# Sliding-window attention beside an S5 scan: the sum over eight shifts moved from VectorE into accumulating DMAs

## The chip, the cores and the metric

The kernel runs on one core of one Trainium2 chip. The metric is device time in microseconds (us); the time before is 157.37 us, the median of three runs (157.35 to 158.69). A run of this kernel is one launch with all inputs and the output in device memory.

The engines have the names of the profile: PE is TensorE (matmuls), PEld its weight loads, DVE is VectorE, ACT is ScalarE, POOL is GpSimd, SP is SyncE. Each engine works through its own queue in order and waits on semaphores for the others. Matmul results lie in PSUM, in eight banks that the kernel hands out one by one.

## The reference, cut to what matters

Two independent parts are put side by side in the output, 448 columns each, for a sequence of 2048 tokens.

```python
# part A: attention over W = 8 earlier tokens, spaced by 2; 16 heads of 28
q, k, v = split(x @ wqkv)
idx = pos[:, None] - 2 * arange(8)[None, :]
logits = einsum("bhsd,bhswd->bhsw", q, k[idx]) * 28 ** -0.5     # masked where idx < 0
attn = softmax(logits)
o = einsum("bhsw,bhswd->bhsd", attn, v[idx])
a = o.reshape(B, S, 448) @ wo
# part B: a diagonal complex state space model (S5)
h[t] = Lam_bar * h[t-1] + B_bar @ x[t]
y = 2 * real(C @ h) + x * Dskip
out = concatenate([a, y], axis=-1)
```

The change concerns the second einsum of part A: for each token and head, eight value vectors ("shifts") are weighted and added up.

## The kernel before, in words

**Layout of part A.** Sixteen neighbouring tokens lie on one partition, so 128 partitions hold all 2048. The keys and values have a halo of 14 tokens copied from the partition before, and a shift by two tokens is then only another offset along the free dimension. Queries, keys and values come from `proj` (L358 to L397), called with a matrix (0 for q, 1 for k, 2 for v), a range of token positions `j`, and a list of functions to be put between the positions. Each position takes three matmuls of 128 rows (L384) and one of 64 rows (L375), the 64-row tile. With `flip=True` the 64-row tiles go first, otherwise last; calls alternate so that 64-row tiles of two calls meet. ACT copies every finished bank to SBUF (L370). The functions in between are transposes of x (`g_xta`), products of the SSM's input weights (`b_weights`, L404, copied by ACT at L406), transposes of B's x (`b_x`, copied at L418), or single ScalarE steps (`act`).

**The value stage.** Tokens are handled in eight pairs, p = 0 to 7. For each pair VectorE multiplies the eight shifted value rows by the attention weights (`pv_mul`, L671): eight slices of 2 x 448 = 896 elements, in one buffer of eight slices or two of four (`where`, L650). Some products are then added together on VectorE (`joins`, L651, L677). `av` (L682 to L702) adds the slices that are left: TensorE multiplies each by an identity matrix, seven matmuls a slice, accumulating in two banks, which also transposes the result. ACT copies the sum to `oTs` (L702). `wo` (L709 to L726) multiplies by the output weights, for two pairs at a time behind av(2), av(4) and av(6), and singly for the pairs 6 and 7 at the end, and stores each half pair (112 KB).

The slices left for TensorE are 4, 6, 6, 7, 7, 7, 8 and 6 for the pairs 0 to 7, 51 in all. VectorE makes ten adds for that: one of four slices (pair 0) and nine of one slice.

**What sets the order.** The order on each engine is the order in which the program issues the instructions. TensorE's is written out by hand. VectorE's work is mostly a list of items with estimated costs (`add`), from which `pe()` and `pump` take items whenever the estimated load of TensorE is ahead. The products of the pairs 4 and 5 lie in the buffers of the SSM state, and wait until its last outputs have been issued (`free`). Pair 6 uses pair 0's buffer again, and pair 7 pair 1's (`pv_ok`).

POOL builds constants early and sets a few masked logits to -1e30 (L597); it issues no DMA in the kernel before. SP issues nearly all DMAs, the stores of the output among them.

Of the kernel before, what the change touches and what calls it, by code (L numbers as in the profile page):

```python
# [10 lines left out]
ALU = mybir.AluOpType  # L11
# [19 lines left out]
def view(ap, offset, dims):  # L31

    return bass.AP(ap.tensor, ap.offset + offset, [list(ap.ap[0])] + [list(d) for d in dims])
# [3 lines left out]
def kernel(  # L37
# [18 lines left out]
    V = nc.vector  # L56
    ACT = nc.scalar
    PE = nc.tensor
    POOL = nc.gpsimd
# [7 lines left out]
    def bank(dt=F32):  # L67
        return psum.tile([128, 512 if dt == F32 else 1024], dt, tag="b", name="b")
# [79 lines left out]
    ident = const.tile([128, 128], BF16, tag="ident")  # L148
# [32 lines left out]
    count = [0, 0, 0]  # L181
# [3 lines left out]
    def add(cost, fn, ok=None):  # L185
        todo.append((cost, fn, ok))
        return todo[-1]

    def pop():
        c, fn, _ = todo.pop(0)  # L190
        fn()
        load[1] += c

    def pump(lead=0.0):
        while (todo and load[1] < load[0] + lead and (todo[0][2] is None or todo[0][2]())
               and (not until or load[1] + todo[0][0] < until[0])):
            pop()
# [14 lines left out]
    def pe(cost):  # L212
        load[0] += cost
        pump(1.0)
# [144 lines left out]
    def proj(t, hi, n, *between, odd=False, flip=False):  # L359


        todo_ = list(between)
        js = range(hi, hi - n, -1)
        pss = {j: bank() for j in js} if flip else {}

        def copy(j):
            src = pss[j][:, 0:D].rearrange("p (h d) -> p d h", h=H)
            dst = (q_s[:, :, j * H:(j + 1) * H] if t == 0 else
                   k_s[:, :, HALO + j, :] if t == 1 else v_s[:, HALO + j])
            ACT.copy(dst, src)  # L370

        def halves_():
            for j in js:
                rows = slice(HS * (j % 2), HS * (j % 2 + 1))
                PE.matmul(pss[j][:, 0:D], xTA[rows, j // 2, 6, :], wts[rows, t, 3, :], start=flip, stop=not flip)  # L375

        if flip:
            halves_()
            pe(0.24)
        for j in js:  # L380
            if not flip:
                pss[j] = bank()
            for kt in range(3):
                PE.matmul(pss[j][:, 0:D], xTA[:, j // 2, 2 * kt + j % 2, :], wts[:, t, kt, :],  # L384
                          start=(kt == 0 and not flip), stop=(kt == 2 and flip))
            if flip:
                copy(j)
            pe(0.56)
            if (odd or j % 2 == 0) and todo_ and j > js[-1]:
                todo_.pop(0)()  # L390
        if not flip:
            halves_()
            for j in js:
                copy(j)
            pe(0.2 + 0.1 * n)
        for fn in todo_:
            fn()  # L397


    def b_weights(t):  # L400
# [242 lines left out]
    PD = 2 * D  # L643
# [4 lines left out]
    spare = (u1[:, 7 * D:7 * D + 4 * PD], wbuf[:, 0:4 * PD], BT.rearrange("p t k n -> p (t k n)"),  # L648
             tab.rearrange("p a t c -> p (a t c)"))
    where = ((kA,), (kB, lB), spare[0:2], spare[2:4], (uA[:, 0:4 * PD], uA[:, 4 * PD:]), (uB,), (kA,), (kB, lB))  # L650
    joins = {(0, 0): 4, (1, 0): 1, (1, 1): 1, (2, 0): 1, (2, 1): 1, (3, 0): 1, (4, 0): 1, (5, 0): 1, (7, 0): 1, (7, 1): 1}  # L651
    steps = [(p, i) for p in range(8) for i in range(len(where[p]))]
    free = []

    def pv_of(i):
        p, k = steps[i]
        buf = where[p][k]
        n = buf.shape[1] // PD
        return buf.rearrange("p (w n) -> p w n", w=n), n, k * n

    def pv_ok(i):
        p, k = steps[i]
        if p in (4, 5):
            return bool(free)
        return p < 4 or count[1] > steps.index((p - 6, k))

    def pv_mul(i, e):
        p, _ = steps[i]
        pv, n, s0 = pv_of(i)
        j = 14 - 2 * p + e  # L670
        V.tensor_tensor(pv[:, :, D * e:D * (e + 1)].rearrange("p w (d h) -> p w d h", h=H),  # L671
                        attn[:, s0:s0 + n, H * j:H * (j + 1)].unsqueeze(2).to_broadcast((128, n, DH, H)),
                        view(v_s, (2 * s0 + j) * D, ((2 * D, n), (H, DH), (1, H))), ALU.mult)
        if e == 1:
            m = joins.get(steps[i], 0)
            if m:
                V.tensor_tensor(pv[:, 0:m], pv[:, 0:m], pv[:, n - m:n], ALU.add)  # L677
            count[0] += 1

    accs = {}  # L680

    def av(i):  # L682
        p, k = steps[i]
        pv, n, s0 = pv_of(i)
        n_add = n - joins.get(steps[i], 0)
        if k == 0:
            accs[p] = [bank(), bank()]
        acc = accs[p]
        end = k == len(where[p]) - 1
        for w in range(n_add):  # L690
            for t in range(7):
                PE.matmul(acc[t // 4][:, 128 * (t % 4):128 * (t % 4 + 1)], pv[:, w, 128 * t:128 * (t + 1)], ident[:],  # L692
                          start=(k == 0 and w == 0 and t % 4 == 0), stop=(end and w == n_add - 1 and t in (3, 6)))
        count[1] += 1
        pe(0.39 * n_add)
        if end:
            o = oTs[p].rearrange("p k n -> p (k n)")
            for b_, (lo, hi) in enumerate(((0, 512), (512, PD))):
                if p == 7 and b_ == 1:
                    V.tensor_copy(o[:, lo:hi], acc[b_][:, 0:hi - lo])  # L700
                else:
                    ACT.copy(o[:, lo:hi], acc[b_][:, 0:hi - lo])  # L702

    wo_p = u1[:, 0:7 * D].rearrange("p (k n) -> p k n", k=7)
    wo_r = A_wo.rearrange("(h d) n -> d h n", h=H)
    oTs = [q_s.rearrange("p d n -> p (d n)")[:, PD * i:PD * (i + 1)].rearrange("p (k n) -> p k n", k=7) for i in range(8)]
    out_a = out[0].rearrange("(p j) n -> j p n", j=J)

    def wo(*ps):  # L709
        pss = {}  # L710
        for p in ps:
            for e in range(2):
                ps_ = pss[p, e] = bank()
                for k in range(3):
                    PE.matmul(ps_[:, 0:D], oTs[p][:, 4 * e + k, :], wo_p[:, 4 * e + k, :], start=(k == 0), stop=False)  # L715
        for p, e in pss:
            rows = slice(HS * e, HS * (e + 1))
            PE.matmul(pss[p, e][:, 0:D], oTs[p][rows, 3, :], wo_p[rows, 3, :], start=False, stop=True)
        for p, e in pss:
            ya = outp.tile([128, D], BF16, tag="yo")  # L720
            if p == 7 and e == 1:
                V.tensor_copy(ya[:], pss[p, e][:, 0:D])
            else:
                ACT.copy(ya[:], pss[p, e][:, 0:D])  # L724
            (ACT if p == 7 and e == 0 else SP).dma_start(out_a[14 - 2 * p + e, :, 0:D], ya[:])
        pe(1.32 * len(ps) + 0.23)  # L726
# [26 lines left out]
    g_xta(7)  # L753
    spin(8)
    proj(1, 15, 4, X(6), both(params_in, params1, X(5)), X(4), odd=True)
    has_tab = list(tables())
    params_act()
    params2()
    add(0.2, params3)
    has_R = [add(0.6, lambda k=k: build_R(k)) for k in range(4)]  # L760
    proj(1, 11, 4, X(3), X(2))
    proj(1, 7, 2, flip=True)
    has_R += [add(0.6, lambda k=k: build_R(k)) for k in range(4, T - 1)]
    proj(0, 15, 4, X(1), X(0))
# [95 lines left out]
    for i in range(len(steps)):  # L860
        for e in range(2):
            n = pv_of(i)[1]
            add(0.09 + 0.233 * n + (0.08 + 0.466 * joins.get(steps[i], 0) if e == 1 else 0.0),
                lambda i=i, e=e: pv_mul(i, e), lambda i=i: pv_ok(i))
            if i == 0 and e == 0:
                add(0.0, sm0[1])
            elif i == 0 and e == 1:
                add(1.6, sm0[2])
# [13 lines left out]
            out_close(j, cb)  # L882

    free.append(True)
    for i, (p, k) in enumerate(steps):
        while count[0] <= i:
            pop()
        pump(7.0)
        av(i)
        if k == len(where[p]) - 1:  # L890
            if p in (2, 4, 6):
                wo(p - 2, p - 1)
            elif p == 7:
                wo(6)
    wo(7)
# [1 line left out]
_INS = ['A_x', 'A_wqkv', 'A_wo', 'B_x', 'B_Lambda_re', 'B_Lambda_im', 'B_B_re', 'B_B_im', 'B_C_re', 'B_C_im', 'B_log_dt', 'B_Dskip']  # L897
# [26 lines left out]
```

## Time and profile before

| | us |
|---|---|
| median of the runs | 157.37 |
| the profiled execution, device time | 157.24 |
| its span in the profile | 155.4 |
| PE busy | 149.7 (96% of the span) |
| DVE busy | 135.3 (87%) |
| ACT busy | 100.4 (65%) |
| POOL busy | 18.1 (12%) |
| chain of waits that ended last | PE 57%, DVE 33%, DMA 5%, issue 2% |

The granted clock of TensorE is full in all 40 slices of the span. In a timeline, each line gives start and duration in us, then engine, line of the program, operation, what is written and read, and how many instructions are merged. Matmuls are pipelined: seven in a row start 0.056 us apart while each lasts 0.219, so the pitch between starts is what a queue of them costs. The windows view gives, for each stretch of time, the busy time and number of instructions of each engine, the granted clock, the mean busy share of the 16 DMA engines, and the GB/s moved.

The end of the span, in the timeline's starts: TensorE begins av(0) at 119.56, the first `wo` at 125.81, the second at 134.15, av(6) at 139.74, the third `wo` at 143.31, av(7) at 146.16, wo(6) at 148.52 and wo(7) at 150.05. VectorE's last product of pair 6 ends at 140.3.

### The profile page before, as it was taken

To read this page: it belongs to the slowest core of one execution; us is meant where nothing else is said; L and a number is where in the kernel's file an instruction comes from. 1 tells how busy PE (TensorE), PEld (TensorE's weight loads), DVE (VectorE), ACT (ScalarE), POOL (GpSimd) and SP (SyncE) were. 2 spreads that over 40 slices of the span, in tenths; PEclk is the share of its full clock that TensorE was granted. 3 is DMA by queue.
4 is the path that set the end of the run, shared out by engine and by line. 5 is a ranking of instruction groups with operands and counts; after the bars stand their busy time and mean duration, and the time that the engine had idled before them with its cause. 6 is when DMAs were issued, how large, how long until landed. Compare 5 with 4: busy or idle time off the path is not lost.

```text
span 155.4 us, 3483 instructions
## 1 busy us (share of the span) xinstructions
PE 149.7 (96%) x1432; PEld 101.5 (65%) x1434; DVE 135.3 (87%) x134; ACT 100.4 (65%) x199; POOL 18.1 (12%) x59
## 2 busy tenths in 40 slices
PE   7999999999999999999999999999999999999990
PEld 7655544465657778787776665666666969778650
DVE  2379888999999999999999999999999999999411
ACT  0349588987988698697468489975444426353541
POOL 4088894000000000000010000000000000000000
PEclk9999999999999999999999999999999999999999
DMA  5999999999894000000000000222452003021033
GB/s 141 241 271 259 194 230 281 211 175 121 170 190 72 0 4 2 0 4 0 0 4 0 0 0 0 90 94 85 143 162 89 30 4 109 15 90 32 10 108 118
DMA packets 21431, 14.57 MB, mean 94 GB/s; under 512 B 8856, under 2 KB 21288, under 8 KB 21288
## 3 DMA queue, kind: packets, MB, share of 16 engines
q1 hardware_dynamic: 20499, 14.05, 38.9%
q10 hardware_dynamic: 916, 0.30, 0.9%
q8 instruction: 11, 0.18, 0.5%
q14 instruction: 5, 0.04, 0.1%
HBM read 7.46 MB, written 3.67 MB: 72 GB/s over the span
## 4 chain that ended last, share of the span: by engine, by line
PE 57%; DVE 33%; DMA 5%; issue 2%; ACT 1%; DVEq 0%; ACTq 0%
PE b L384 17%; PE b L449 11%; DVE u L671 6%; DVE k_s L671 6%; DMA u<-in_A_x_dram 5%; PE b L468 4%; PE b L375 4%; PE b L692 4%; PE b L715 3%; PE b L459 3%; DVE u L576 2%; PE b L404 2%; DVE k_s L677 2%; PE b L352 2%; PE b L413 1%
## 5 line engine op out<-in xcount | busy, mean ns | idle before, releaser
L576 DVE TENSOR_TENSOR u<-q_s,k_s 128x7168 bf16<-128x7168 bf16 (+1 forms) x10 | 31.2, 3139 | 0.2
L384 PE MATMUL b<-wbuf,u 128*128 128x448 bf16 x144 | 30.6, 353 | 0.1
L384 PEld LDWEIGHTS <-u 128*128 128x128 bf16 x144 | 12.9, 98 | 12.2 <-issue 2.0
L449 PE MATMUL b<-xT,BT 128*128 128x256 bf16 x168 | 20.6, 273 | 0.0
L469 ACT CAST u<-b 128x512 bf16<-128x512 f32 (+1 forms) x32 | 15.6, 548 | 5.2 <-PE b L468 5.1
L449 PEld LDWEIGHTS <-BT 128*128 128x128 bf16 x168 | 16.2, 98 | 2.0
L579 DVE TENSOR_TENSOR u<-u 128x3584 bf16<-128x3584 bf16 (+1 forms) x10 | 16.4, 1648 | 0.2
L531 ACT CAST u<-b 128x512 bf16<-128x512 f32 (+1 forms) x28 | 13.5, 546 | 3.0 <-PE b L530 2.9
L542 PE MATMUL b<-Cw,u 128*128 128x448 bf16 x64 | 14.7, 352 | 0.0
L702 ACT CAST q_s<-b 128x512 bf16<-128x512 f32 (+1 forms) x15 | 7.4, 539 | 10.5 <-PE b L692 10.5
L556 ACT CAST yo<-b 128x448 bf16<-128x448 f32 x16 | 8.3, 528 | 8.9 <-PE b L554 4.5
L671 DVE TENSOR_TENSOR k_s<-u,v_s 128x3584 bf16<-128x3584 bf16 (+1 forms) x8 | 12.0, 1551 | 0.0
L724 ACT CAST ya<-b 128x448 bf16<-128x448 f32 x15 | 7.0, 544 | 7.0 <-issue 5.4
L554 PE MATMUL b<-Cw,u 128*128 128x448 bf16 x48 | 11.4, 353 | 0.0
L671 DVE TENSOR_TENSOR u<-u,v_s 128x1792 bf16<-128x1792 bf16 (+1 forms) x8 | 10.1, 1317 | 0.0
L597 POOL MEMSET u<- 1x128 bf16 (+3 forms) x10 | 1.3, 162 | 75.2 <-DVE u L593 53.9
L715 PE MATMUL b<-u,q_s 128*128 128x448 bf16 x48 | 9.9, 353 | 0.0
L528 PE MATMUL b<-u,ident 128*128 128x512 bf16 (+1 forms) x28 | 9.9, 353 | 0.0
L530 PE MATMUL b<-u,R 128*128 128x255 bf16 x49 | 9.6, 273 | 0.0
L370 ACT CAST k_s<-b 128x448 bf16<-128x448 f32 x16 | 7.4, 547 | 3.1 <-PE b L375 3.1
L370 ACT CAST q_s<-b 128x448 bf16<-128x448 f32 x16 | 7.9, 564 | 2.2 <-PE b L375 2.0
L418 ACT COPY xT<-b 128x896 bf16<-128x896 bf16 x8 | 7.5, 945 | 2.8 <-PE b L415 2.8
(161 smaller groups left out, 276.0 us busy)
## 6 DMA issues: line engine op xcount, KB each, us to landing
out_dram<-yo SPq DMA_DIRECT2D x16, 112.0 KB
out_dram<-ya SPq DMA_DIRECT2D x15, 112.0 KB
u<-in_B_x_dram SPq DMA_DIRECT2D x2, 768.0 KB
u<-in_A_x_dram SPq DMA_DIRECT2D x3, 384.0 KB
wbuf<-in_A_wqkv_dram SPq DMA_DIRECT2D x3, 336.0 KB
k_s<-k_s SPq DMA_DIRECT2D x1, 784.0 KB
v_s<-v_s SPq DMA_DIRECT2D x1, 784.0 KB
u<-in_A_wo_dram SPq DMA_DIRECT2D x6, 112.0 KB
```

What stands on the lines that cost most here:

```text
L370: ACT.copy(dst, src)
L384: PE.matmul(pss[j][:, 0:D], xTA[:, j // 2, 2 * kt + j % 2, :], wts[:, t, kt, :], start=(kt == 0 and not flip), stop=(kt == 2 and flip))
L449: PE.matmul(ps[:, i * NC:(i + 1) * NC], BT[:, t, kt, :], xT[:, jp, 2 * kt + jj, :], start=(kt == 0 and i == 0), stop=False)
L469: ACT.copy(Z[:, pr_[0]:pr_[0] + n, j, :], ps[:, 0:n * NC].rearrange("p (t c) -> p t c", t=n))
L528: PE.matmul(ps[:, 0:n * NC], ident[:], Z[:, sl, j, :], start=True, stop=False)
L531: ACT.copy(Z[:, sl, j, :], ps[:, 0:n * NC].rearrange("p (t c) -> p t c", t=n))
L542: PE.matmul(ps[:, 0:D], Z[:, t, j, cols], Cw[:, t, :], start=(t == 0), stop=False)
L554: PE.matmul(ps[:, 0:D], Z[:, t, j, cols], Cw[:, t, :], start=False, stop=(t == NT - 1))
L576: V.tensor_tensor(pr[:, w:w + n], qv, kv, ALU.mult)
L579: V.tensor_tensor(pr[:, w:w + n, 0:14, :], pr[:, w:w + n, 0:14, :], pr[:, w:w + n, 14:28, :], ALU.add)
L671: V.tensor_tensor(pv[:, :, D * e:D * (e + 1)].rearrange("p w (d h) -> p w d h", h=H), attn[:, s0:s0 + n, H * j:H * (j + 1)].unsqueeze(2).t ...
L715: PE.matmul(ps_[:, 0:D], oTs[p][:, 4 * e + k, :], wo_p[:, 4 * e + k, :], start=(k == 0), stop=False)
```

## The change

1. For the pairs 1 to 6, once all eight products are there, a DMA issued by POOL adds the last four slices to the first four in SBUF (`accum_op=ALU.add`), and TensorE sums four slices. The pairs 0 and 7 keep eight slices. VectorE adds none any more.
2. `av` is called once for a pair in place of once for a buffer, and starts when all of the pair is there.
3. In `proj`, without `flip`, the functions not yet called are called ahead of the 64-row tiles and the copies, in place of behind them. This concerns five calls: proj(1, 11) with X(2), proj(0, 15) with X(0), proj(1, 5) with an `act`, proj(2, 7) with BW(3), and proj(0, 7) with BX(0, 1) and BW(6).

```diff
@@ proj
+        for fn in todo_:
+            fn()
         if not flip:
             halves_()
             for j in js:
                 copy(j)
             pe(0.2 + 0.1 * n)
-        for fn in todo_:
-            fn()
@@ the value stage
-    joins = {(0, 0): 4, (1, 0): 1, (1, 1): 1, (2, 0): 1, (2, 1): 1, (3, 0): 1, (4, 0): 1, (5, 0): 1, (7, 0): 1, (7, 1): 1}
+    joined = range(1, 7)
...
-        return p < 4 or count[1] > steps.index((p - 6, k))
+        return p < 4 or count[1] > p - 6
...
         if e == 1:
-            m = joins.get(steps[i], 0)
-            if m:
-                V.tensor_tensor(pv[:, 0:m], pv[:, 0:m], pv[:, n - m:n], ALU.add)
             count[0] += 1
+            if p in joined and i + 1 == len(steps) or p in joined and steps[i + 1][0] > p:
+
+                lo, hi = terms(p)[0:4], terms(p)[4:8]
+                for a_, b_ in runs(lo, hi):
+                    POOL.dma_start(a_, b_, accum_op=ALU.add, max_dma_last_dim=4 * PD)
+
+    def terms(p):
+        return [(buf, w) for buf in where[p] for w in range(buf.shape[1] // PD)]
+
+    def runs(lo, hi):
+        (la, l0), (ha, h0) = lo[0], hi[0]
+        return [(la[:, l0 * PD:(l0 + 4) * PD], ha[:, h0 * PD:(h0 + 4) * PD])]
...
+    def av(p):
+        acc = [bank(), bank()]
+        all_ = terms(p)[0:4] if p in joined else terms(p)
+        for w, (buf, u) in enumerate(all_):
             for t in range(7):
+                PE.matmul(acc[t // 4][:, 128 * (t % 4):128 * (t % 4 + 1)], buf[:, u * PD + 128 * t:u * PD + 128 * (t + 1)], ident[:],
+                          start=(w == 0 and t % 4 == 0), stop=(w == len(all_) - 1 and t in (3, 6)))
...
-            add(0.09 + 0.233 * n + (0.08 + 0.466 * joins.get(steps[i], 0) if e == 1 else 0.0),
+            add(0.09 + 0.233 * n,
...
-    for i, (p, k) in enumerate(steps):
-        while count[0] <= i:
+    for p in range(8):
+        while count[0] <= steps.index((p, len(where[p]) - 1)):
             pop()
         pump(7.0)
-        av(i)
+        av(p)
```

Here `PD` is 896, the elements of one slice.

More of the change, by code (lines that the diff above doesn't have):

```diff
@@ L674, in pv_mul @@
         if e == 1:
-            m = joins.get(steps[i], 0)
-            if m:
-                V.tensor_tensor(pv[:, 0:m], pv[:, 0:m], pv[:, n - m:n], ALU.add)
             count[0] += 1
-    accs = {}
[L682 to L690, printed above, removed]
+            if p in joined and i + 1 == len(steps) or p in joined and steps[i + 1][0] > p:
+                lo, hi = terms(p)[0:4], terms(p)[4:8]
+                for a_, b_ in runs(lo, hi):
+                    POOL.dma_start(a_, b_, accum_op=ALU.add, max_dma_last_dim=4 * PD)
@@ L691, in av @@
+    def terms(p):
[3 more added lines that the diff above has]
+        return [(la[:, l0 * PD:(l0 + 4) * PD], ha[:, h0 * PD:(h0 + 4) * PD])]
+    accs = {}
+    def av(p):
+        acc = [bank(), bank()]
+        all_ = terms(p)[0:4] if p in joined else terms(p)
+        for w, (buf, u) in enumerate(all_):
             for t in range(7):
-                PE.matmul(acc[t // 4][:, 128 * (t % 4):128 * (t % 4 + 1)], pv[:, w, 128 * t:128 * (t + 1)], ident[:],
-                          start=(k == 0 and w == 0 and t % 4 == 0), stop=(end and w == n_add - 1 and t in (3, 6)))
+                PE.matmul(acc[t // 4][:, 128 * (t % 4):128 * (t % 4 + 1)], buf[:, u * PD + 128 * t:u * PD + 128 * (t + 1)], ident[:],
+                          start=(w == 0 and t % 4 == 0), stop=(w == len(all_) - 1 and t in (3, 6)))
@@ L694, in av @@
         count[1] += 1
[L695 to L702, printed above, removed]
+        pe(0.39 * len(all_))
+        o = oTs[p].rearrange("p k n -> p (k n)")
+        for b_, (lo, hi) in enumerate(((0, 512), (512, PD))):
+            if p == 7 and b_ == 1:
+                V.tensor_copy(o[:, lo:hi], acc[b_][:, 0:hi - lo])
+            else:
+                ACT.copy(o[:, lo:hi], acc[b_][:, 0:hi - lo])
@@ L884 @@
     free.append(True)
-    for i, (p, k) in enumerate(steps):
-        while count[0] <= i:
+    for p in range(8):
+        while count[0] <= steps.index((p, len(where[p]) - 1)):
             pop()
         pump(7.0)
-        av(i)
[L890 to L894, printed above, removed]
+        av(p)
+        if p in (2, 4, 6):
+            wo(p - 2, p - 1)
+        elif p == 7:
+            wo(6)
     wo(7)
```

## The prediction

> **What bounds the kernel now.** First the slices of the span, for the engines that matter.
>
> ```profile
> PE   7999999999999999999999999999999999999990
> DVE  2379888999999999999999999999999999999411
> ```
>
> TensorE and VectorE are both full from slice 7 to slice 37, so neither alone is the bound. Then the end of the chain of waits (start, duration, what):
>
> ```profile
> 136.42 3.88 DVE k_s L671 x2
> 140.30 0.05 issue
> 140.34 3.13 PE b L692 x53
> ```
>
> Up to 140.3 the chain runs on VectorE's products, then TensorE takes over with av(6) and keeps it. TensorE's own timeline shows how little it waits for that:
>
> ```profile
> 119.56 2.90 PE L692 MATMUL b<-ident,k_s 128*128 128x128 bf16 x49
> ...
> 140.34 3.13 PE L692 MATMUL b<-ident,k_s 128*128 128x128 bf16 x53 [0.27 <-DVE k_s L671]
> ...
> 148.52 1.30 PE L715 MATMUL b<-u,q_s 128*128 128x448 bf16 x6
> ```
>
> From 119.56 to 148.52 it idles only at 140. So in the value stage a gain needs less work on both engines, and the change has that. VectorE's timeline there:
>
> ```profile
> 108.21 2.02 DVE L677 TENSOR_TENSOR k_s<-k_s 128x3584 bf16<-128x3584 bf16 x1
> ...
> 113.94 0.62 DVE L677 TENSOR_TENSOR k_s<-k_s 128x896 bf16<-128x896 bf16 x1
> ...
> 125.14 2.09 DVE L671 TENSOR_TENSOR tab<-u,v_s 128x1792 bf16<-128x1792 bf16 x2
> 127.14 2.08 DVE L671 TENSOR_TENSOR u<-u,v_s 128x1792 bf16<-128x1792 bf16 x2
> ```
>
> The adds are the L677 lines. Two products without an add behind them take 2.00 us from start to start (125.14 to 127.14); with one they take 2.66 (111.82 to 114.48 in the same timeline), so a small add costs 0.66.
>
> **The change, part by part.** The sum stands against the profiled execution, 157.24 us, a span of 155.4 with 1.8 around it; the median is 0.13 above.
>
> *TensorE, removed and added.* 51 slices become 8 + 6 x 4 + 8 = 40. The first 49 matmuls start over 2.74 us (119.56 to 122.30), 0.056 each, 0.39 a slice. Eleven slices fewer save 4.30; with the waits at 140, 4.76 at best. In starts, if nothing waits: av(0) 119.56, av(1) 122.69, av(2) 124.25, wo(0,1) 125.82, av(3) 128.67, av(4) 130.23, wo(2,3) 134.65 less 2.85 = 131.80, av(5) 134.65, av(6) 136.21, wo(4,5) 137.78, av(7) 140.63, wo(6) 143.76 in place of 148.52 (2.85 is a `wo` of two pairs, 143.31 to 146.16). ACT's two copies after an av (0.97) and four after a `wo` (1.84) still fit behind the next av's 1.56 or two of them.
>
> *VectorE, removed.* The add of pair 0 (1.94, 108.21 to 110.15) and seven small ones before the end of pair 6: 1.94 + 7 x 0.66 = 6.56. Pair 6's products end at 140.30 - 6.56 = 133.74 and, at 4.0 us a pair, pairs 1 to 5 at 113.7, 117.7, 121.7, 125.7 and 129.7; pair 7's at 137.7, ahead of av(7). Pair 4 starts at 121.7, after the SSM's last read of its buffer at 119.56.
>
> *The new wait.* Behind av(p) in TensorE's in-order queue stand everything later, the `wo` products and av(7), and ACT's copies and SP's stores follow those. POOL has nothing queued behind its DMAs but the next ones. The slack from the end of the products to the unhindered av is 9.0, 6.6, 7.0, 4.5, 5.0 and 2.5 us for the pairs 1 to 6. Pair 6 is the tight one: from av(6) to wo(6) it is 1.56 + 2.85 + 3.13 = 7.54, so wo(6) is back at 148.52 when av(6) starts at 140.98. With a latency of 2.5 the gain is whole, at 7.2 it is gone, and beyond it every us is lost.
>
> *The latency.* No accumulating DMA and none from POOL is in the trace. Each moves 128 x 3584 x 2 bytes = 917.5 KB. The nearest rows (us; busy time of PE, PEld, DVE, ACT, POOL; clock, DMA share, GB/s):
>
> ```profile
> 40.00:46.00 6.00, 6.00 (x55) 3.35 (x53) 5.83 (x5) 5.59 (x14) 0.00 (x0) 1.00 1.09 211
> ...
> 114.00:120.00 6.00, 6.00 (x51) 3.67 (x49) 5.93 (x8) 2.16 (x6) 0.00 (x0) 1.00 0.29 96
> 130.00:134.00 4.00, 4.00 (x76) 4.00 (x74) 4.00 (x4) 1.43 (x4) 0.00 (x0) 1.00 0.35 117
> ```
>
> At 40 to 46 the halo of the values is copied from SBUF to SBUF, the engines saturated, at 211 GB/s: 4.35 us for 917.5 KB. At 130 to 134 four stores move 468 KB in 0.35 x 4 = 1.4 us of engine time, 334 GB/s: 2.75 us. If the sum needs a second full pass for the destination, the halo's rate gives 8.7. So 2.75 to 8.7; I take 4.35, from the only row that goes from SBUF to SBUF, between the store's rate with two passes (5.5) and with one.
>
> Here a rule bears. "Collectives: The Full Stack" of the Trainium skill, section "The bandwidth ceiling", says that an adding DMA reads two sources on one read ring and so runs at half a copy's rate, 15.5 GB/s an engine by its figures: an estimate of 3.7 us here. With it the sum below would be some 4 us shorter, the lower end of the forecast; no run so far shows it.
>
> For issue and landing I take 1 us each: the wait of SP's queue for the last store is 1.4 at its longest, transfer (0.35) included. Bounds 1 to 4 together.
>
> *Queueing.* 4.35 is above VectorE's 4.0 a pair, and the stores use the same 16 engines: 0.29 x 6 = 1.7 until 120, some 0.4 just after, and 1.4 for each `wo` of two pairs, of which the first surely lies before pair 6's turn and the second half so. Starting at 114.7, six transfers and 4.2 of stores end at 114.7 + 26.1 + 4.2 = 145.0; landed 146.0. Then wo(6) begins at 153.5, 5.0 late.
>
> *The functions ahead of the 64-row tiles.* Four of the five moved functions hold TensorE work; its queue is full here, so its delay comes through to the end.
>
> ```profile
> 42.97 0.55 PE L375 MATMUL b<-wbuf,u 64*128 64x448 bf16 x4
> ...
> 44.40 0.55 PE L375 MATMUL b<-wbuf,u 64*128 64x448 bf16 x4
> ```
>
> Between the two groups stand BX(0,1) and BW(6). Moved ahead, they leave the groups adjacent: eight in a row take 0.87 (at 28.66) against 2 x 0.48, so about 0.1 is saved at each of four places. But the cover goes: two of the four banks that the second group opens are ones ACT has just copied, and the work in between hid those copies (0.42 us apart at 43.36). If they are the banks of the first group's tiles, the stall is 0.5, 0.6 and 1.2 at proj(0,15), proj(2,7) and proj(0,7): +2.2 in all. If they are the moved function's own, the only late one is BW(6)'s copy, queued behind an xT copy (0.80 pitch): +0.4 less 0.3. Banks came free in the order of ACT's copies so far, so I take +0.1; bounds -0.4 to +2.2. X(2) and X(0) need no later load than the transposes before them; the `act` only changes ACT's order, in a gap of 0.9 us.
>
> Sum: 157.24 + 5.0 + 0.1 = 162.3, 162.5 beside the median.
>
> **The rivals.** *Short latency.* If an accumulation runs at the stores' 334 GB/s, nothing queues, and pair 6 lands 1 + 2.75 + 1 = 4.75 after 133.74, at 138.5: wo(6) at 146.0, 2.5 early, 154.9 with the 0.1, and never below 157.24 - 4.76 - 0.4 = 152.1. It decides where the latency stays under about 5.5. For it: the DMA share is only 0.29 to 0.35 in this stage. Against: the halo's rate, and a sum that must also read its destination.
>
> *About even.* Engine time of 3.3 to 4.0 keeps up with VectorE, and the latency of 5.7 to 8.7 that issue, stores and landing make of it leaves 156 to 159. A way into this case: POOL's issue waits for the VectorE instruction that is running, at most 2.0 us (the 128x3584 product), which makes 154.9 into 156.9. "SBUF — State Buffer" of the Trainium skill, section "SBUF: two separate sides", tells of such a lock for descriptors that POOL writes while VectorE is in a two-port mode; the same page says that tensor_tensor has none, so I give it little.
>
> *Two passes.* With 8.7 a transfer, six end at 114.7 + 52.2 + 4.2 = 171.1: 26 later than in the forecast, 188.
>
> *TensorE's stalls early.* The +2.2 above on top of any case.
>
> **How the numbers follow.** Forecast (transfers queue, 159 to 168): 0.50. Short latency: 0.28. Even: 0.14. Two passes: 0.08. Within 1% is 155.8 to 158.9, about what a measurement here can tell from no change: faster 0.28, same 0.14, slower 0.58. The forecast's own range is 159 to 168 (3.7 to 5.2 an accumulation, with the early stalls). Leaving out the two passes, the best end of the short latency and a little above 168 makes two in ten: 154.5 to 168.
>
> **What would show it.** Right: TensorE idle at L692 waiting for a DMA, growing from av(2) or av(3) on, and a DMA share near 1 from 115 to 145. Matmuls at L692 must be 280, L677 gone, and VectorE's last product near 138. A DMA share well under 1 with the same waits would mean latency or POOL's issue and not engine time. Wrong: no wait ahead of av(6), or L375 followed by gaps near 19, 36 or 44 that add over 1 us.

## The result and the profile after

The changed kernel takes 169.15 us (median of four runs, 168.64 to 169.82); beside it on the same chip the kernel before takes 158.03. The ratio is 1.070 with a 95% interval of 1.062 to 1.078: slower, as forecast, and 1.2 us above the upper end of the range. The profiled execution takes 169.43 us with a span of 167.7; before it was 157.24 and 155.4. (In six of the profiled executions, this one among them, VectorE waits 1.3 to 3.0 us for the copy of the keys' halo, here 1.4 us. Here nothing of it is left in the value stage: av(0) begins at 121.00, and at 121.19 with the moves alone, where that wait is absent. From the other five only distances are used.)

The 40 slices of the span, for the engines that changed, with the granted clock and the share of the DMA engines:

```profile
PE   7999799999999999999999999999991995919990
DVE  1289879997899999999999999999999991000011
PEclk9999999999999999999999999999998589975898
DMA  5999999997980000000000012245999999981023
```

TensorE, which was full up to slice 38, has three holes: slices 30, 33 and 35. VectorE is done with its products by slice 33; it has lost its adds. The DMA engines are full from slice 28 to slice 34; their share from 118 to 150 us was 0.17 before. And the granted clock, full in every slice before, drops to a half behind two of the holes. TensorE's timeline shows the same in microseconds (start and duration; in brackets the idle time and what ended it):

```profile
121.00 4.85 PE L696 MATMUL b<-ident,k_s 128*128 128x128 bf16 x84
129.59 3.14 PE L696 MATMUL b<-ident,u 128*128 128x128 bf16 x28 [3.73 <-DMA u<-wbuf]
...
140.47 1.72 PE L696 MATMUL b<-ident,u 128*128 128x128 bf16 x28 [1.89 <-DMA u<-u]
...
145.27 1.72 PE L696 MATMUL b<-ident,u 128*128 128x128 bf16 x28 [0.32 <-DMA u<-u]
150.57 3.15 PE L696 MATMUL b<-ident,k_s 128*128 128x128 bf16 x28 [3.58 <-DMA k_s<-k_s]
...
160.72 1.30 PE L718 MATMUL b<-u,q_s 128*128 128x448 bf16 x6
```

The 84 matmuls at 121.00 are av(0) with eight slices and av(1) with four, so the first accumulation was in time. From av(2) on TensorE waits for DMAs: 3.73, 1.89, 0.32 and 3.58 us. The 28 matmuls of av(6) take 3.15 where the same 28 take 1.72 at 145.27: half speed. wo(6), at 148.52 before, begins at 160.72, 12.2 later, and that is the whole difference between the profiled executions. The end of the chain of waits (start, duration, what) names the transfer, from its issue to its landing, the moment at which its semaphore tells that all of it has arrived:

```profile
131.70 1.19 POOL u L680
...
135.33 15.11 DMA k_s<-k_s
...
150.57 3.15 PE b L696 x28
```

15.11 us pass between the issue of pair 6's accumulation and its landing. That is not the time of one transfer. The table of DMA issues (number, KB each, us from issue to landing) shows how it grows:

```profile
u<-u POOLq DMA_DIRECT2D x2, 896.0 KB, 12.9
...
k_s<-l POOLq DMA_DIRECT2D x1, 896.0 KB, 7.5
u<-wbuf POOLq DMA_DIRECT2D x1, 896.0 KB, 9.9
BT<-tab POOLq DMA_DIRECT2D x1, 896.0 KB, 12.8
```

Pair 1 (`k_s<-l`) lands after 7.5, pair 2 (`u<-wbuf`) after 9.9, pair 3 (`BT<-tab`) after 12.8, the pairs 4 and 5 (`u<-u`) after 12.9 as a median, pair 6 after 15.1: each stands in line behind those before it. The windows (from and to; length; busy time and instructions of PE, PEld, DVE, ACT, POOL; granted clock, DMA share, GB/s) show that the line is at the DMA engines:

```profile
118.00:150.00 32.00, 23.04 (x251) 16.88 (x249) 21.04 (x18) 9.44 (x20) 5.97 (x5) 0.88 1.06 205
...
130.00:132.00 2.00, 2.00 (x22) 2.00 (x21) 2.00 (x2) 0.00 (x0) 0.30 (x1) 0.50 1.06 186
...
152.00:154.00 2.00, 2.00 (x19) 1.78 (x17) 0.00 (x0) 0.73 (x3) 0.00 (x0) 0.50 0.23 72
```

For 32 us all 16 engines are taken (1.06) and move 205 GB/s, while TensorE is busy for 23.04 of them. The kernel before has TensorE busy for 31.73 us of the same stretch:

```profile
118.00:150.00 32.00, 31.73 (x426) 25.02 (x423) 27.93 (x28) 13.94 (x29) 0.00 (x0) 1.00 0.17 56
```

### The profile page after: what moved, and what is told of

It is laid out like the page before. It is cut to its first block, busy times and chain, and to the rows that moved or that the text cites. A ratio compares the mean times of both kernels' runs of the same rounds, so it can differ in the third digit from the quotient of the medians.

```text
span 167.7 us, 3347 instructions
## 1 busy us (share of the span) xinstructions
PE 151.4 (90%) x1355; PEld 101.7 (61%) x1357; DVE 127.7 (76%) x124; ACT 100.6 (60%) x199; POOL 25.2 (15%) x65
## 3 DMA queue, kind: packets, MB, share of 16 engines
HBM read 7.46 MB, written 3.67 MB: 66 GB/s over the span
## 4 chain that ended last, share of the span: by engine, by line
PE 67%; DMA 13%; DVE 8%; ACT 4%; issue 4%; POOL 3%; POOLq 0%; DVEq 0%; ACTq 0%
PE b L384 13%; PE b L449 10%; DMA k_s<-k_s 9%; PE b L542 7%; PE b L554 5%; DMA u<-in_A_x_dram 4%; DVE u L671 4%; PE b L696 4%; PE b L468 4%; PE b L718 3%; PE b L530 3%; PE b L528 3%; PE b L459 2%; PE b L375 2%; PE b L545 2%
## 5 line engine op out<-in xcount | busy, mean ns | idle before, releaser
L384 PEld LDWEIGHTS <-u 128*128 128x128 bf16 x144 | 12.9, 98 | 14.0 <-issue 4.0
L703 DVE CAST q_s<-b 128x384 bf16<-128x384 f32 x1 | 0.6, 558 | 21.9 <-PE b L696 21.9
L696 PE MATMUL b<-ident,k_s 128*128 128x128 bf16 x140 | 9.7, 238 | 3.6 <-DMA k_s<-k_s 3.6
L718 PE MATMUL b<-u,q_s 128*128 128x448 bf16 x48 | 12.6, 420 | 0.0
L696 PE MATMUL b<-ident,u 128*128 128x128 bf16 x84 | 6.6, 249 | 6.0 <-DMA u<-wbuf 3.7
L696 PEld LDWEIGHTS <-k_s 128*128 128x128 bf16 x140 | 9.2, 108 | 4.3 <-issue 4.1
L554 PE MATMUL b<-Cw,u 128*128 128x448 bf16 x48 | 11.4, 353 | 0.0
L696 PEld LDWEIGHTS <-u 128*128 128x128 bf16 x84 | 6.1, 113 | 6.7 <-DVE u L671 3.9
## 6 DMA issues: line engine op xcount, KB each, us to landing
u<-u POOLq DMA_DIRECT2D x2, 896.0 KB, 12.9
```

The source lines that it names most:

```text
L554: PE.matmul(ps[:, 0:D], Z[:, t, j, cols], Cw[:, t, :], start=False, stop=(t == NT - 1))
L696: PE.matmul(acc[t // 4][:, 128 * (t % 4):128 * (t % 4 + 1)], buf[:, u * PD + 128 * t:u * PD + 128 * (t + 1)], ident[:], start=(w == 0 and ...
```

## The experiments

The theory after the result had four parts: the accumulating DMAs run one after another at about 5 us each against VectorE's 4 us a pair; TensorE's idling then costs it its clock; the moved functions cost a stall early in the kernel; nothing else matters. The rivals were that POOL's issue or the latency of its DMAs is the cost, whatever is added, that the moves are the cost, and that the clock only follows from the waits and has no price of its own. The kernel before took 157.3 to 157.4 beside each experiment, and the ratios are to those runs.

**The moves alone.** The kernel before with change 3 only:

```diff
+        for fn in todo_:
+            fn()
         if not flip:
             halves_()
...
-        for fn in todo_:
-            fn()
```

> The kernel before with the moved functions alone, joins on VectorE as before. My theory, read from the changed kernel's trace: the second 64-row group at proj(0,15) waits 1.26 us for VectorE's copy of X(0), which stands behind VectorE's other work, and nothing else of it costs much; TensorE starts av(0) about 1.4 us late, at 121.0 in place of 119.56, and the end follows: 158.5 to 159.2. Rival, as predicted: ACT's copies are the stall (0.5, 0.6 and 1.2 us at three places), or nothing is (+0.1): then 157.4.

Measured: 158.87 us (158.84 to 159.03), a ratio of 1.010 [1.009, 1.012]. Its TensorE early on:

```profile
18.64 1.04 PE L375 MATMUL b<-wbuf,u 64*128 64x448 bf16 x7
20.93 0.35 PE L375 MATMUL b<-wbuf,u 64*128 64x448 bf16 x1 [1.26 <-DVE u L355]
```

and its VectorE at that time:

```profile
18.65 0.62 DVE L355 COPY u<-b 128x896 bf16<-128x896 bf16 x1
19.19 1.16 DVE L234 TENSOR_TENSOR R<-dup,coef 128x896 bf16<-128x896 bf16 x2
20.27 0.61 DVE L355 COPY u<-b 128x896 bf16<-128x896 bf16 x1
```

Seven of the eight adjacent 64-row matmuls run through, the last waits 1.26 us until VectorE has copied the transposes of X(0). That copy was issued behind two products for the SSM's tables (1.16 us). The waiting matmul, of position 8, reads nothing of X(0); by the program it can only be the bank that it waits for. Before, X(0) came last, and nobody wanted its bank so soon. ACT's fourth copy ends at the same time (20.87), but the semaphores in the trace rule it out: the seventh and the eighth matmul wait for the one that VectorE's copies of X(1) and X(0) update at their ends (19.27 and 20.88), and ACT's copies update another. The seventh starts at 19.33, when ACT, which began at 19.03, hasn't finished its first copy of these tiles. VectorE's products in the value stage come 1.63 us later than before (pair 1's first starts at 113.45, not 111.82): the stall goes through to the end on both engines.

**The DMAs alone.** The changed kernel with change 3 taken back, run twice, as e2 and as e9:

```diff
-        for fn in todo_:
-            fn()
         if not flip:
             halves_()
...
+        for fn in todo_:
+            fn()
```

> The changed kernel with the functions back behind the 64-row tiles: the accumulating DMAs alone. Theory: six transfers run one after the other from the end of pair 1's products on, so all of the stage moves by the 1.4 us of the early stall and nothing else: 167.7, wo(6) about 1.4 us sooner than 160.72. Rival: the start is hidden behind the queue of transfers and nothing comes of it: 169.1.

> The accumulating DMAs alone, once more, on the same chip as e10_warm_shorter, for its profile: the landing of pair 6's transfer, the granted clock behind it, and the time from that landing to wo(6). 165.5 to 167, wo(6) 9 to 10 us behind the landing if the clock falls for av(6) and the wo behind it, 7.6 to 8.2 if it falls only in part.

Measured: 166.89 us (ratio 1.058 [1.053, 1.063]) and 168.35 (1.067 [1.062, 1.072]). Over the kernel before, the DMAs alone cost 9.6 and 10.9 us. The second run misses its expected 165.5 to 167 and lies 1.46 above the first. A late copy of the halo isn't the reason, since the profiled execution of the second (168.31 us) has no wait there. In it wo(6) begins at 159.55, 10.4 behind the landing of pair 6 at 149.15 where 9 to 10 were expected. So 11.0 of the 12.2 us are the DMAs', and 1.2 are what the moves, and whatever else differs between the two executions, add in the changed kernel's profile:

```profile
149.28 3.14 PE L696 MATMUL b<-ident,k_s 128*128 128x128 bf16 x28 [3.47 <-DMA k_s<-k_s]
...
159.55 1.30 PE L718 MATMUL b<-u,q_s 128*128 128x448 bf16 x6
```

In the first one's profiled execution the same stretch is shorter:

```profile
153.02 3.09 PE L696 MATMUL b<-ident,k_s 128*128 128x128 bf16 x28 [3.38 <-DMA k_s<-k_s]
...
161.94 1.30 PE L718 MATMUL b<-u,q_s 128*128 128x448 bf16 x6
```

From av(6) to wo(6) it takes 8.92 there and 10.27 in the second. The granted clock stays at 0.50 for 3.4 us there (152.5 to 155.9) and for 6.8 us in the second (148.1 to 154.9). This 1.35 is near the 1.46 between the medians; that it makes the difference was not shown, since the other executions have no profile.

**X(0) put back alone.** The kernel before with change 3 for all calls but proj(0, 15):

```diff
-    def proj(t, hi, n, *between, odd=False, flip=False):
+    def proj(t, hi, n, *between, odd=False, flip=False, late=False):
...
+        if not late:
+            for fn in todo_:
+                fn()
         if not flip:
             halves_()
...
-        for fn in todo_:
-            fn()
+        if late:
+            for fn in todo_:
+                fn()
...
-    proj(0, 15, 4, X(1), X(0))
+    proj(0, 15, 4, X(1), X(0), late=True)
```

> The kernel before with the moved functions, but X(0) left behind the 64-row tiles of proj(0, 15). Theory: the 1.26 us wait there is all that the moves cost, and the other three places save 0.1 each: 157.0 to 157.3. Rival: other places cost too (ACT's copies at proj(2, 7) and proj(0, 7)): 157.6 or more.

Measured: 157.77 us, a ratio of 1.001 [0.998, 1.005]. With X(0) back between them, the two groups of 64-row matmuls run without a wait:

```profile
18.35 0.55 PE L375 MATMUL b<-wbuf,u 64*128 64x448 bf16 x4
...
19.33 0.55 PE L375 MATMUL b<-wbuf,u 64*128 64x448 bf16 x4
```

The median lies in the rival's range, but the kernel before took 157.43 beside it, and the interval leaves 0.8 us at most for the other places. So X(0) is all that can be measured of the moves; the saving of 0.1 at each place isn't seen in the time, nor the stalls behind ACT's copies.

**The same DMAs without the addition.** The DMAs-alone kernel with `accum_op` dropped, so that POOL, the queue, the bytes and the waits stay and only the addition goes, and with it the first four shifts of six pairs from the result:

```diff
-                    POOL.dma_start(a_, b_, accum_op=ALU.add, max_dma_last_dim=4 * PD)
+                    POOL.dma_start(a_, b_, max_dma_last_dim=4 * PD)
```

> As the accumulating DMAs alone, but each of the six DMAs only copies the last four slices over the first four, from POOL as well (the six pairs then sum four shifts twice left out: the first four are missing from the result). If reading the destination as well is what makes a transfer 5.0 us, a copy takes 2.7 to 4.4, keeps up with VectorE's 4.0 a pair, and the kernel is at 155 to 160. If the path through POOL or from SBUF to SBUF is what limits, it stays 4.8 or more and the time within 2 us of the accumulating one.

Measured: 154.6 us, a ratio of 0.983 [0.981, 0.985], just below what was expected. The time from issue to landing no longer grows:

```profile
u<-u POOLq DMA_DIRECT2D x2, 896.0 KB, 4.4
...
k_s<-l POOLq DMA_DIRECT2D x1, 896.0 KB, 4.5
```

And the engines are not full (same columns as above):

```profile
118.00:138.00 20.00, 18.70 (x241) 14.34 (x239) 19.78 (x17) 10.36 (x22) 3.63 (x5) 1.00 0.76 288
```

So it is neither POOL's issue nor the latency of a POOL DMA: with those in place the kernel is 2.7 us faster than before. The single packets in the DMA records of this trace and of the changed kernel's give the rates:

| | packet | its time (median) | an engine | first packet to end of the last |
|---|---|---|---|---|
| plain copy | 7168 bytes | 286 ns | 25 GB/s | 2.45 to 2.82 us |
| accumulation | 3584 bytes | 313 ns | 11.4 GB/s | 5.1 to 5.4 us, 6.0 and 6.2 where stores run beside it |

The addition makes the same 917.5 KB take about twice as long: 5.24 us, the mean of the four with the fewest stores beside them, against 2.60, the mean of the six copies. Sixteen packets an engine at 313 ns are 5.0 us, and at that pace one follows the other in the line. How much of it is the second read and how much the smaller packets, which come with the addition, was not tried. "Collectives: The Full Stack" of the Trainium skill, section "The bandwidth ceiling", has half a copy's rate for the adding step of a ring between cores, which reads two sources: this ratio agrees. The 15.5 GB/s an engine that the prediction works out from that page's figures doesn't hold here, where 11.4 was measured; the measurement decides.

**Half the size.** As the DMAs-alone kernel, but only the last two slices are added to the two before them, and TensorE sums six (52 slices in all, one more than before):

```diff
-        all_ = terms(p)[0:4] if p in joined else terms(p)
+        all_ = terms(p)[0:6] if p in joined else terms(p)
...
-                lo, hi = terms(p)[0:4], terms(p)[4:8]
+                lo, hi = terms(p)[4:6], terms(p)[6:8]
...
-        return [(la[:, l0 * PD:(l0 + 4) * PD], ha[:, h0 * PD:(h0 + 4) * PD])]
+        return [(la[:, l0 * PD:(l0 + 2) * PD], ha[:, h0 * PD:(h0 + 2) * PD])]
```

> As the accumulating DMAs alone, but each adds only the last two slices to the two before them, and TensorE sums six: half the bytes a transfer, 52 slices on TensorE (12 more than with four, one more than before the change). Theory (a transfer costs engine time by its bytes, 5.0 us for four slices, and they queue only where that exceeds VectorE's 4.0 a pair): 2.5 us each, no queue, pair 6 lands about 5 us after its products, TensorE never waits long, the clock stays at 1.00: 157 to 158.5. Rival (a fixed cost for each of the six DMAs, from POOL or the landing, is what queues): the transfers still end near 148, 164 or more.

Measured: 157.49 us, a ratio of 1.002 [0.999, 1.005]. The accumulations land 4.4 to 5.4 us after their issue, with no line growing, and TensorE never waits:

```profile
118.00:140.00 22.00, 22.00 (x302) 17.77 (x301) 20.40 (x17) 9.30 (x21) 4.28 (x5) 1.00 0.74 157
```

TensorE is busy for 22.00 of 22.00 us. A transfer of 2.5 to 2.9 us from its first packet to the end of the last (3.6 for pair 6, with stores beside it) against VectorE's 4 keeps up, but with 52 slices on TensorE nothing is gained. So what decides is the DMA time of a pair against VectorE's time of a pair.

**The clock.** The DMAs-alone kernel, in which TensorE does matmuls of zeros into a spare bank in place of idling: e4 with 55, 55 and 75 of them ahead of av(2), av(4) and av(6), e10 with 50, 50 and 62:

```diff
+        if p in (2, 4, 6):
+            keep = bank()
+            for _ in range({2: 55, 4: 55, 6: 75}[p]):
+                PE.matmul(keep[:, 0:128], zero[:], zero[:], start=True, stop=True)
         av(p)
```

> As the accumulating DMAs alone, but TensorE runs 55, 55 and 75 matmuls of zeros ahead of av(2), av(4) and av(6), about 3.1, 3.1 and 4.2 us, while it waits. Theory: the granted clock stays at 1.00 to the end, av(6) and the wo behind it take 1.56 and 2.85 in place of 2.94 and 4.07, and the kernel is 2.6 us faster than without them. Rival: the clock falls for another reason (DMA load), and the time is the same or longer.

> As e9_dma_alone_again, with 50, 50 and 62 matmuls of zeros ahead of av(2), av(4) and av(6), so that they end ahead of the landings (75 ended 1.2 us behind). Theory of the clock: granted 1.00 to the end, wo(6) 8.2 us behind the landing of pair 6 (7.54 and 0.6 from landing to the first matmul), 1.4 to 2.6 us faster than without. Rival: the clock was a sign and no cost, the time is the same within 0.5.

Measured: 167.66 us (1.066 [1.058, 1.074]) and 167.62 (1.062 [1.054, 1.070]), against 166.89 and 168.35 without the zeros. Of the 2.6 us that were expected, and the 1.4 to 2.6, the totals show nothing: the runs of one of these kernels lie up to 2.4 us apart (166.38 to 168.79 in e10), and in e4 the 75 matmuls end 1.2 us after the last packet of pair 6 (151.17), so they take back part of the gain. The stage itself is readable. TensorE in e4, and a window (columns as above):

```profile
148.18 4.35 PE L895 MATMUL b<-zero 128*128 128x128 bf16 x75
152.37 1.73 PE L696 MATMUL b<-ident,k_s 128*128 128x128 bf16 x28
...
159.92 1.30 PE L718 MATMUL b<-u,q_s 128*128 128x448 bf16 x6
...
126.00:151.00 25.00, 21.67 (x317) 18.14 (x315) 13.87 (x11) 7.31 (x15) 3.57 (x3) 1.00 1.06 205
```

With the DMA engines as full as in the changed kernel (1.06) the clock stays at 1.00, so it is TensorE's idling that lowers it and not the load of the DMA engines. From av(6) to wo(6) it takes 159.92 - 152.37 = 7.55 at full clock (the same in e10), against 159.55 - 149.28 = 10.27 in e9, where the clock is at 0.50 until 154.9. The lost clock therefore costs 2.7 us in the last stretch alone, and 1.4 in the profiled execution of e2 (8.92). That a kernel with the accumulations can keep those 2.7 in its whole time was not shown.

**Only what the DMA engines can carry.** The kernel before, with accumulating DMAs for some of the sums only, and VectorE's small adds moved to the later pairs; e6 with two DMAs (`sums_ = {(0, 0): 4, (1, 1): 2}`, 48 slices), e8 with three (47 slices):

```diff
-    joins = {(0, 0): 4, (1, 0): 1, (1, 1): 1, (2, 0): 1, (2, 1): 1, (3, 0): 1, (4, 0): 1, (5, 0): 1, (7, 0): 1, (7, 1): 1}
+    joins = {(2, 0): 1, (2, 1): 1, (4, 0): 1, (4, 1): 1, (5, 0): 2, (6, 0): 1, (7, 0): 1, (7, 1): 1}
+    sums_ = {(0, 0): 4, (1, 1): 2, (3, 1): 2}
...
+            m = sums_.get(steps[i], 0)
+            if m:
+                buf = where[p][steps[i][1]]
+                POOL.dma_start(buf[:, 0:m * PD], buf[:, (n - m) * PD:n * PD], accum_op=ALU.add, max_dma_last_dim=4 * PD)
...
-        n_add = n - joins.get(steps[i], 0)
+        n_add = n - joins.get(steps[i], 0) - sums_.get(steps[i], 0)
```

> The kernel before, with an accumulating DMA where there is time for it: pair 0 (four slices, products 11 us ahead of av(0)) and two slices of pair 1; VectorE's time so freed goes into more adds for the pairs 3, 4 and 5. 48 slices on TensorE in place of 51 (-1.2 us with 0.39 a slice), VectorE -1.4. Theory: the two transfers land before av(0) and av(1), and the kernel is 1.2 to 1.6 us faster: 155.7 to 156.1. Rival (any latency of such a DMA shows up as a wait of TensorE): 157.3 or more.

> As e6_two_pairs, and two slices of pair 3 by a DMA too, an add more for pair 6: 47 slices, VectorE -2.1. Theory: pair 3's products are done near 123, landed at 128.1, just ahead of av(3) at 128.6: 155.2 to 155.6. Rival: 5 us of latency is already too late there, a wait of 1 us or more at av(3), and it is no better than e6_two_pairs.

Measured: 156.2 us, 0.1 above what was expected, a ratio of 0.990 [0.986, 0.993], and 155.5 us (155.32 to 155.73), 0.987 [0.984, 0.990]. The second is the fastest that computes the whole reference, ahead of both kernels. POOL issues its three DMAs at 109.01, 114.39 and 123.97. They land at 118.6, 122.8 and 129.9, and TensorE reads those sums at 119.79, 122.92 and 130.47:

```profile
119.79 3.29 PE L697 MATMUL b<-ident,k_s 128*128 128x128 bf16 x56
...
130.47 0.94 PE L697 MATMUL b<-ident,tab 128*128 128x128 bf16 x14
...
146.74 1.30 PE L720 MATMUL b<-u,q_s 128*128 128x448 bf16 x6
```

From first packet to last they take 5.9, 5.7 and 4.1 us, though the second and third have half the bytes: beside stores half the size didn't take half the time. The second lands just 0.2 us before it is read. No matmul waits, and wo(6) begins 1.78 us ahead of the kernel before: four slices fewer at 0.39 and no wait of 0.27 for VectorE would make 1.83.

## Why the prediction was right or wrong

Its forecast was "transfers queue", and that is what happened. What failed is the sum from pair 1's products to wo(6): it had no term for the clock, and too little for the issue and for the transfer. It came out 7.2 us short at wo(6). By its own terms, in the profiled execution:

| step | forecast | measured | difference |
|---|---|---|---|
| pair 1's products end | 113.7 | 115.27 | +1.57 |
| from there to the first packet | 1.0 | 2.58 | +1.58 |
| six transfers and the stores among them | 30.3 | 32.03 | +1.73 |
| end of the last transfer to av(6) | 1.0 | 0.69 | -0.31 |
| av(6) to wo(6) | 7.54 | 10.15 | +2.61 |
| wo(6) begins | 153.54 | 160.72 | +7.18 |

**TensorE's saving: right.** 40 slices are left. In the copies without addition, where nothing holds it up before wo(0,1), that `wo` starts 6.25 us behind av(0) (119.72 to 125.97); the forecast was 6.26. The matmuls at L696 are 280.

**VectorE's saving: right.** From pair 1's products to pair 7's it takes 3.96 a pair (115.27 to 139.04) against the 4.0 of the forecast. Of the 1.57 at the start, 1.14 are gone in the second run of the DMAs alone (114.13), which has neither the moves nor the wait at the halo.

**The new wait and the break-even: right.** TensorE waits at the accumulated pairs, in line with the forecast that six transfers don't fit beside VectorE's pace, and the time from issue to landing grows from pair to pair. The waits themselves don't grow from pair to pair, as the sign of being right had it: they are 3.73, 0, 1.89, 0.32 and 3.58 us for the pairs 2 to 6. The copies without addition also price the rival "short latency" well: it was to give 154.9, and 154.6 was measured with transfers of 2.60 as a mean and landings 4.1 to 4.5 us after issue.

**The transfer: mis-sized, and near by luck.** The forecast took 4.35 from the halo's copy, as one pass. In the line an accumulation takes 5.0: a copy of this form takes 2.6, and the addition about doubles it. So the row it relied on was near the value by chance, being slow for a copy; why it is slow wasn't tried. The right pair of terms was in the text, the store's rate (2.75) with two passes (5.5), and the value was taken below it. The stores were over-priced in turn: 32.03 less six times 5.01 (16 packets of 313 ns) is 2.0, not 4.2. The two errors (+4.0, -2.2) make up the +1.73.

**Issue and landing: mis-sized.** 1.58 of the miss is the way from the products to the first packet. Its pieces in POOL's timeline are 0.60 until POOL starts and 1.41 for the issue:

```profile
115.87 1.41 POOL L680 DMA_DIRECT2D k_s<-l  x1 [12.74 <-DMA out_dram<-yo]
```

and then 0.57 until the first packet at 117.85. Only the first one counts, since the others are issued while the line is still busy. That POOL would be held up by VectorE, the way into "about even", isn't seen: it starts 0.3 to 0.6 us behind each pair's last product, in the middle of VectorE's next one, which takes 1.1 to 2.0 us.

**The clock: the missing term.** The largest part, 2.61, had no line in the forecast at all. It worked with the durations of before, 7.54 from av(6) to wo(6), taken at full clock, for a stage in which it had itself put TensorE to idle for microseconds. With the clock kept up, the experiments have 7.55 there, so the 2.61 is the clock's. "TensorE: Matmul & The Clock Gate" of the Trainium skill, section "Part 1: The HAM clock gate (the "warmup" mystery)", has the clock halved behind an idle window of about 3.4 us; the trace agrees, with 0.50 behind idle times of 3.73 and 3.58 us and a full clock behind 1.89.

**The functions ahead of the 64-row tiles: the wrong copy.** The forecast weighed ACT's copies and named BW(6)'s as the only late one among the moved functions' own; X(0)'s, which VectorE makes, was left out. It was the one: 1.26 us at 20.73 in the changed kernel, which "gaps near 19 that add over 1 us" was to show. The sum of +0.1 was wrong, the bound of +2.2 holds it. At proj(2, 7) and proj(0, 7) the eight adjacent matmuls take 1.09 and 1.45 in place of 0.93, where the 0.6 and 1.2 of that bound would have been lost: small, and not seen in the time once X(0) is back.

## What to carry to other kernels

A DMA that adds took about twice as long here as a plain copy of the same bytes: price it so, and compare the time of one with the pace at which they are issued, not with the mean load of the DMA engines. Where each is done before the next is issued they hold up nobody, as at half the size; above that pace every one pushes the next, and the last one's delay is the whole sum. And where a new wait leaves TensorE idle for some 3.5 us, ask what the clock will do to the work behind it: here that was 1.4 to 2.7 us on top of the wait, in a term that the forecast didn't have. When work is moved, ask of every bank it opens which engine empties it and what stands in that engine's queue.

## What the runs showed of the hardware

- Accumulating DMAs of one POOL queue run one after the other: the first packets of each follow the last ones of the one before, and the DMA share stays at 1.00 to 1.09 while only 205 GB/s move; the packets are of half the size of a plain copy's (3584 in place of 7168 bytes) and last longer (313 against 286 ns).
- POOL is taken for 1.19 to 1.42 us by the issue of an accumulation of four slices, 0.85 to 1.07 by one of two slices, and 0.72 to 0.94 by a plain copy of four.
- The granted clock, once at 0.50, stayed there for 6.8 us in the changed kernel (128.7 to 135.5 and 149.1 to 156.0), though TensorE was busy from 129.59 and from 150.57 on; behind waits of about the same length (3.67 and 3.38 us) it stayed there for only 3.4 us in the profiled execution of e2 (132.0 to 135.5 and 152.5 to 155.9). What decides between the two was not tried.
